# Loading q, k and v with casting DMAs instead of casting them on GpSimd and VectorE

## The chip, the cores and the metric

The kernel runs on one core of one Trainium2 chip. The metric is the device time of one execution in microseconds (us), lower is better. Every time below is a median of executions. Kernels are compared only within the same rounds. A ratio is the mean time of one kernel's runs over that of the other's of the same rounds, so it is not quite the ratio of the medians quoted.

Names of the engines: PE is TensorE (matmuls), PEld its weight loads, DVE is VectorE, ACT is ScalarE, POOL is GpSimd, SP is SyncE.

## The reference

Eight batches of sliding-window attention with an ALiBi bias feed an RWKV channel mix. Cut to what matters:

```python
# q, k, v: (8 batches, 8 heads, 576 positions, 64), float32
scores = q @ k.T / 8 ; scores += -slope[h] * |i - j| ; keep 0 <= i - j < 128
attn = softmax(scores) ; x = attn @ v            # -> (8, 576, 512)
xk = mu_k * x + (1 - mu_k) * x_prev               # x_prev: x of the position before
xr = mu_r * x + (1 - mu_r) * x_prev
out = sigmoid(xr @ w_r) * (relu(xk @ w_k) ** 2 @ w_v)   # w_k 512x1024, w_v 1024x512
```

## The kernel before

The work is cut into 32 iterations, four pairs of heads for each of eight batches. Iterations 0 to 3 (batch 0) have their own code; from iteration 8 on, one loop does everything. In an iteration TensorE transposes q and k of a later pair, computes the scores, ScalarE takes the exponential, VectorE multiplies it by a table of `exp(bias)` and zeros (the "mask multiply"), TensorE multiplies by v (`av`), VectorE normalises (`xu`), TensorE transposes back (`outT`), and VectorE mixes with the position before (`dl`, `xk`, `xr`). Matmuls of the channel mix fill the rest of TensorE's time as `units`.

The inputs come in fp32 by plain DMAs from SyncE. GpSimd casts q and v to bf16, and VectorE casts k:

```python
def cast_qk(it, part=None, fq=pool_cast, fk=vec_cast):
    cs = csp.tile([128, 2, NF, 2, D], BF16, tag="cs", name="cs", bufs=4)
    ...
    for i, f in ((0, fq), (1, fk)):            # q on GpSimd, k on VectorE
        f(cs[:, i, 0:r1 - r0]..., ldr[:, i, it % NBUF]...)

def cast_v(it, j0=0, j1=NF):
    pool_cast(vs_buf[it % NBUF]..., vdr[:, it % NBUF, :, j0:j1])

def feed(it, fk=vec_cast):
    cast_qk(it, None, pool_cast, fk)
    cast_v(it)
    load_qk(it + 4)                            # plain DMAs, rows of 1 KB
    load_v(it + 4)
    if it % G == 0:
        load_tail(it // G + 1)                 # positions 512 to 575
```

The multiply, and the place of `feed` in the loop:

```python
# scores():
nc.scalar.activation(out=ah, in_=sa[:, :, 0:w], func=AF.Exp, scale=float(scale))
if not early:
    nc.vector.tensor_tensor(out=ah, in0=ah,
                            in1=mask[:, 2 * g:2 * g + 2, m0:m0 + w], op=ALU.mult)

# ahead of the loop
feed(2 * G + 2)
...
for it in range(2 * G, NIT + 2):
    scores_full(it)
    run_units(bud * .3)
    if it > 2 * G:
        av(it - 1, 0, NJ)                      # frees at and vs of iteration it - 1
    run_units(bud * .3)
    ...
    transp(it + 2)                             # ends in ScalarE's copy of qk
    feed(it + 3)
    ...
    outT(it - 1, 0, NJ)
```

The order of TensorE, SyncE and GpSimd in the loop is the order of the program; that of VectorE and ScalarE is chosen by the scheduler.

The softmax here doesn't subtract the row's maximum and nothing guards it: scores larger than these inputs give would overflow.

## Time and profile before

The kernel took 274.94 us, the median of three runs (273.6 to 275.26). The profiled run spans 272.5 us. TensorE is busy nearly all the time, and VectorE is second:

| | before |
|---|---|
| TensorE busy | 244.9 us of 272.5 (90%) |
| VectorE busy | 211.4 us (78%) |
| ScalarE, GpSimd busy | 179.9 us, 74.0 us |
| first transposes of iterations 4, 8, 9, 12, 28 | 41.1, 55.4, 67.4, 86.2, 202.2 us |
| mask multiply, mean of 34 in 90 to 210 us | 1048 ns |

The row of first transposes is when TensorE starts the first transpose matmul of an iteration, read from the list of TensorE's instructions in the trace. Four iterations are one batch, so the time from iteration 12 to 28 over four is the steady period: (202.2 - 86.2) / 4 = 29.0 us.

First, the page of the kernel before: busy time of each engine, two rows of the busy tenths in 40 slices (each digit is one slice of about 6.8 us), and the queue of the DMAs that GpSimd issues (packets, MB, share of 16 engines).

```profile
PE 244.9 (90%) x2272; PEld 145.0 (53%) x2304; DVE 211.4 (78%) x428; ACT 179.9 (66%) x293; POOL 74.0 (27%) x121
...
PE   4589899857999899999999999999999999999994
...
PEclk9999999977999999999999999999999999999999
...
q0 software_dynamic: 2160, 2.63, 5.8%
```

TensorE is full from the eleventh slice on. In slices 9 and 10 (about 55 to 68 us) it is at 5 and 7 tenths, and the clock that it was granted falls below 0.8. The windows view splits that stretch at the first transposes of iterations 8, 9 and 12; its columns are the stretch, its length, the busy time and count of each engine, the granted clock (1 is full), the DMA share and the rate.

```profile
core 0: us, PE busy (x) PEld busy (x) DVE busy (x) ACT busy (x) POOL busy (x), PEclk, DMA share, GB/s
55.40:67.40 12.00, 7.32 (x77) 4.84 (x78) 9.39 (x19) 4.23 (x5) 2.84 (x5) 0.72 0.92 241
67.40:86.20 18.80, 17.69 (x174) 10.71 (x175) 15.73 (x30) 14.42 (x21) 3.73 (x6) 1.00 0.71 194
```

Iteration 8 takes 12.00 us for 7.32 us of TensorE work at a clock of 0.72; the next three together take 18.80 us at full clock. The timeline of that stretch (start, duration, engine, line, operation, tiles; in brackets the idle time before it and what ended it) shows what TensorE stood still for:

```profile
55.46 0.68 DVE L130 CAST cs<-ldr 128x512 bf16<-128x512 f32 x1 [3.98 <-DMA ldr<-in_k_dram]
56.06 0.44 DVE L298 TENSOR_TENSOR dl<-xt 128x576 bf16<-128x576 bf16 x1
...
57.27 0.81 DVE L300 SCALAR_TENSOR_TENSOR xr<-dl,mur_sb,xt 128x576 bf16<-128x576 bf16 x1
...
58.46 0.82 DVE L270 TENSOR_TENSOR xu<-sa,rc 128x640 bf16<-128x640 f32 x1
...
59.34 0.71 PE L284 MATMUL to<-ident,xu 128*128 128x128 bf16 x5 [3.30 <-DVE xu L270]
```

VectorE ran these in the order of its queue: ScalarE's copy `xt`, which `dl` reads, was done at 53.59, but the k cast ahead of it waited for a DMA until 55.46. So `dl`, `xr` and `xu` behind it come late, and TensorE stands still 3.30 us for `xu`.

The view of waits of TensorE's weight loads adds such waits up over 90 to 206 us (line, what it waited for: us in total, times, longest):

```profile
PEld L284 <- DVE xu L270: 5.1, 11, 0.6
PEld L262 <- issue: 4.8, 10, 0.6
PEld L312 <- issue: 2.8, 5, 0.7
PEld L341 <- DVE kk L318: 1.6, 3, 0.7
```

The lines that end in "issue" wait for nothing that the profile shows. The two that name VectorE come to 6.7 us.

### The profile page before, as it was taken

Reading aid. Unit: us, or ns where it says so; the run is one execution under the profiler, and the core shown is the slowest. Engines: PE = TensorE matmul, PEld = TensorE weight load, DVE = VectorE, ACT = ScalarE, POOL = GpSimd, SP = SyncE. Lnnn points to the kernel's source line nnn. Section 1 sums busy time; section 2 is a strip of 40 time slices with the busy share of each in tenths; the row PEclk is TensorE's granted clock in tenths of the full one; section 3 lists DMA queues with packets and bytes.
Section 4 is the critical chain, followed back from the end, with each engine's and each line's share of the span. In section 5 each row is a group of like instructions: output and inputs, shape, how many; then the busy total and the mean of one; then the engine's idle time right before and its main releaser. Section 6 shows DMA issues by size and latency. Waiting matters only on the chain.

```text
span 272.5 us, 6003 instructions
## 1 busy us (share of the span) xinstructions
PE 244.9 (90%) x2272; PEld 145.0 (53%) x2304; DVE 211.4 (78%) x428; ACT 179.9 (66%) x293; POOL 74.0 (27%) x121
## 2 busy tenths in 40 slices
PE   4589899857999899999999999999999999999994
PEld 1245665525555565545555755555565755455461
DVE  2268973367878999998988899989888888976342
ACT  5468688832795776876686677866685868635350
POOL 5383066513042225222320225222422100000000
PEclk9999999977999999999999999999999999999999
DMA  6999999998593691791686551972501211022122
GB/s 164 226 206 196 241 246 283 247 295 196 160 282 85 177 265 45 191 243 50 195 207 161 154 161 58 232 196 91 177 2 38 81 38 41 0 81 77 38 79 77
DMA packets 73229, 40.77 MB, mean 150 GB/s; under 512 B 48112, under 2 KB 68080, under 8 KB 73200
## 3 DMA queue, kind: packets, MB, share of 16 engines
q1 hardware_dynamic: 71040, 37.76, 51.8%
q0 software_dynamic: 2160, 2.63, 5.8%
q8 instruction: 18, 0.29, 0.5%
q14 instruction: 11, 0.09, 0.1%
HBM read 33.56 MB, written 9.44 MB: 158 GB/s over the span
## 4 chain that ended last, share of the span: by engine, by line
PE 54%; DVE 15%; ACT 11%; DMA 8%; SPq 5%; issue 5%; POOL 2%; DVEq 0%; POOLq 0%; ACTq 0%
PE pv L341 17%; PE ps L312 14%; PE pr L327 8%; PE sa L262 5%; DMA ldr<-in_k_dram 4%; DVE at L235 4%; ACT at L233 4%; ACT xt L289 3%; PE tp L184 3%; DVE xk L300 2%; DMA vdr<-in_v_dram 2%; ACT rl L316 2%; PE sa L230 2%; DVE xr L300 2%; DMA tq<-in_k_dram 2%
## 5 line engine op out<-in xcount | busy, mean ns | idle before, releaser
L312 PE MATMUL ps<-xk,wk_sb 128*128 128x256 bf16 (+2 forms) x413 | 70.7, 313 | 3.9 <-ACT rl L316 1.5
L341 PE MATMUL pv<-wv_sb,kk 128*128 128x512 bf16 x271 | 68.8, 382 | 1.8 <-issue 0.6
L233 ACT ACTIVATE at<-sa 128x1024 bf16<-128x1024 f32 (+1 forms) x68 | 63.7, 983 | 9.3 <-PE sa L230 9.1
L316 ACT ACTIVATE rl<-ps 128x256 bf16<-128x256 f32 (+2 forms) x104 | 47.8, 478 | 22.1 <-PE ps L312 14.3
L126 POOL TENSOR_SCALAR vs<-vdr 128x512 bf16<-128x512 f32 (+1 forms) x36 | 24.6, 686 | 127.8 <-issue 89.6
L312 PEld LDWEIGHTS <-wk_sb 128*128 128x128 bf16 x416 | 38.6, 97 | 25.3 <-issue 6.1
L235 DVE TENSOR_TENSOR at<-at,mask 128x1024 bf16<-128x1024 bf16 x48 | 44.6, 968 | 0.8 <-ACT at L233 0.8
L318 DVE TENSOR_TENSOR kk<-rl 128x256 bf16<-128x256 bf16 (+2 forms) x104 | 35.6, 362 | 10.8 <-ACT rl L316 8.6
L341 PEld LDWEIGHTS <-kk 128*128 128x128 bf16 x288 | 26.1, 98 | 27.8 <-DVE kk L318 2.0
L332 ACT ACTIVATE rs<-pr 128x512 bf16<-128x512 f32 x36 | 21.7, 606 | 24.2 <-PE pr L327 24.2
L347 DVE SCALAR_TENSOR_TENSOR ot<-rs,pv 128x512 f32<-128x512 bf16 x36 | 24.3, 674 | 16.8 <-PE pv L341 16.3
L327 PE MATMUL pr<-wr_sb,xr 128*128 128x512 bf16 x132 | 35.7, 379 | 0.7
L187 ACT COPY qk<-tp 128x1024 bf16<-128x1024 bf16 x28 | 28.4, 1016 | 10.9 <-PE tp L184 10.6
L126 POOL TENSOR_SCALAR cs<-ldr 128x512 bf16<-128x512 f32 (+1 forms) x38 | 29.5, 777 | 7.7 <-DMA ldr<-in_q_dram 6.7
L262 PEld LDWEIGHTS <-at 128*128 128x128 bf16 x576 | 23.8, 102 | 11.9 <-issue 7.6
L300 DVE SCALAR_TENSOR_TENSOR xk<-dl,muk_sb,xt 128x576 bf16<-128x576 bf16 (+2 forms) x36 | 27.1, 753 | 1.2
L300 DVE SCALAR_TENSOR_TENSOR xr<-dl,mur_sb,xt 128x576 bf16<-128x576 bf16 (+2 forms) x36 | 27.3, 759 | 0.0
L298 DVE TENSOR_TENSOR dl<-xt 128x576 bf16<-128x576 bf16 (+2 forms) x36 | 15.8, 440 | 9.6 <-ACT xt L289 9.3
L270 DVE TENSOR_TENSOR xu<-sa,rc 128x640 bf16<-128x640 f32 x28 | 22.7, 814 | 0.3
L262 PE MATMUL sa<-vs,at 128*128 128x65 bf16 x448 | 19.7, 196 | 2.3 <-ACT at L233 1.6
L230 PE MATMUL sa<-qk 64*128 64x256 bf16 (+1 forms) x264 | 21.2, 268 | 0.6 <-ACT qk L200 0.2
L130 DVE CAST cs<-ldr 128x512 bf16<-128x512 f32 (+1 forms) x30 | 12.4, 414 | 11.9 <-DMA ldr<-in_k_dram 11.9
(56 smaller groups left out, 217.3 us busy)
## 6 DMA issues: line engine op xcount, KB each, us to landing
out_dram<-ot SPq DMA_DIRECT2D x36, 256.0 KB, 2.1
ldr<-in_q_dram SPq DMA_DIRECT2D x29, 256.0 KB, 4.2
ldr<-in_k_dram SPq DMA_DIRECT2D x29, 256.0 KB, 4.5
vdr<-in_v_dram SPq DMA_DIRECT2D x56, 128.0 KB, 3.9
vdr<-in_v_dram SPq DMA_DIRECT2D x4, 256.0 KB, 5.6
tq<-in_q_dram SPq DMA_DIRECT2D x8, 128.0 KB, 4.8
tq<-in_k_dram SPq DMA_DIRECT2D x8, 128.0 KB, 4.9
tv<-in_v_dram SPq DMA_DIRECT2D x8, 128.0 KB, 4.9
```

The costliest lines, as they stand in the source:

```text
L126: nc.gpsimd.tensor_scalar(out=dst, in0=src, scalar1=1.0, scalar2=0.0, op0=ALU.mult, op1=ALU.add)
L187: nc.scalar.copy(out=qk_buf[it % NBUF].rearrange("p t (c r) -> p t c r", r=NF), in_=tp.rearrange("p (t r c) -> p t c r", t=2, r=NF))
L230: nc.tensor.matmul(sa[:, hl, c0:c0 + n], lhsT=kk_, rhs=qq_, start=not early, stop=True, skip_group_check=True)
L233: nc.scalar.activation(out=ah, in_=sa[:, :, 0:w], func=AF.Exp, scale=float(scale))
L235: nc.vector.tensor_tensor(out=ah, in0=ah, in1=mask[:, 2 * g:2 * g + 2, m0:m0 + w], op=ALU.mult)
L262: nc.tensor.matmul(a5[:, hl, t - t0], lhsT=at[:, lo:lo + 128], rhs=vs[:, u, hl, :] if u < NF else tvb[:, 2 * g + hl], start=(u == us[0]), ...
L300: nc.vector.scalar_tensor_tensor(out=dst[:, g, S * e + c0:S * e + c1], in0=dl[:, 0:c1 - c0], scalar=mu[:, g:g + 1], in1=xp, op0=ALU.mult, ...
L312: nc.tensor.matmul(ps[:, 0:n], lhsT=wk_sb[:, po, 128 * fo:128 * fo + 128], rhs=xk[:, po, c0:c1], start=(po == 0), stop=(po == NPO - 1))
L316: nc.scalar.activation(out=rl[:, 0:n], in_=ps[:, 0:n], func=AF.Relu, scale=RELU_SCALE)
L318: nc.vector.tensor_tensor(out=kk[:, fo, 0:n], in0=rl[:, 0:n], in1=rl[:, 0:n], op=ALU.mult)
L327: nc.tensor.matmul(pr, lhsT=xr[:, po, 128 * c:128 * c + 128], rhs=wr_sb[:, po], start=(po == 0), stop=(po == NPO - 1))
L341: nc.tensor.matmul(pv, lhsT=kk[:, fo, o:o + 128], rhs=wv_sb[:, fo], start=(fo == 0), stop=(fo == NFO - 1))
```

## The change

From batch 1 on, q, k and v are loaded by DMAs that cast on the way, issued by GpSimd straight into bf16 buffers of a whole batch. The intent is to take the casts off GpSimd and VectorE. The Trainium skill, "DMA: Bandwidth & Descriptors", section "SWDGE vs HWDGE vs iDMA", gives the reason for the engine: a cast during a DMA is to be had only from GpSimd. The diff, cut to its core:

```diff
-    vs_buf = [cst.tile([128, NF, 2, W], BF16, name=f"vs{i}") for i in range(NBUF)]
+    vs_buf = [cst.tile([128, NF, H, W], BF16, name=f"vs{i}") for i in range(2)]
+    cb_buf = [ldr....bitcast(BF16)[...] for i in range(2)]     # q and k of a batch
...
+    def cast_load_qk(b, i):
+        hs = (q, k)[i][b, :, 0:SM].rearrange("h (p r) d -> p h r d", p=128)
+        for r in range(NF):
+            nc.gpsimd.dma_start(out=cb_buf[b % 2][:, i, r], in_=hs[:, :, r])
+
+    def cast_load_v(b):
+        for j in range(NF):
+            nc.gpsimd.dma_start(out=vs_buf[b % 2][:, j, :, 0:D],
+                in_=v[b, :, 128 * j:128 * j + 128].rearrange("h p d -> p h d"))
+        ...                                    # and the tails, positions 512 to 575
...
     def transp(it):
-        cs = T.pop(("cs", it, None))
+        cs = cb_buf[b % 2]
...
-    def feed(it, fk=vec_cast):
-        cast_qk(it, None, pool_cast, fk)
-        cast_v(it)
-        load_qk(it + 4)
-        load_v(it + 4)
-        ...
+    def feed(b, g):
+        if g == 1:
+            cast_load_v(b + 1)
+        if g == 2:
+            cast_load_qk(b + 2, 0)
+        if g == 3:
+            cast_load_qk(b + 2, 1)
+            cast_load_tail(b + 2)
...
-    feed(2 * G + 2)
```

Each of these DMAs moves 128 partitions x 8 heads = 1024 rows of 64 values, 256 bytes read and 128 written.

More of the change, by code (lines that the diff above doesn't have):

```diff
@@ L52 @@
     cst = ctx.enter_context(tc.tile_pool(name="cst", bufs=1))
-    tlp = ctx.enter_context(tc.tile_pool(name="tlp", bufs=2))
+    tlp = ctx.enter_context(tc.tile_pool(name="tlp", bufs=1))
     csp = ctx.enter_context(tc.tile_pool(name="csp", bufs=3))
@@ L69 @@
     qk_buf = [cst.tile([128, 2, SM], BF16, name=f"qk{i}") for i in range(NBUF)]
-    vs_buf = [cst.tile([128, NF, 2, W], BF16, name=f"vs{i}") for i in range(NBUF)]
+    vs_buf = [cst.tile([128, NF, H, W], BF16, name=f"vs{i}") for i in range(2)]
+    cb_buf = [ldr.rearrange("p i s h c -> p (i s h c)").bitcast(BF16)[:, 4096 * i:4096 * i + 4096].rearrange("p (i r h d) -> p i r h d", i=2, r=NF, h=H) for i in range(2)]
     at_buf = [cst.tile([128, 2 * 1024 + 64], BF16, name=f"at{i}") for i in range(NBUF)]
@@ L98, in load_qk, with cast_load_tail @@
             dst = ldr[:, i, s0:s0 + npair].rearrange("p s h c -> p (s h) c")
-            if part is None:
-                nc.sync.dma_start(
-                    out=dst,
-                    in_=hs[:, 0:SM].rearrange("h (p r) d -> p h (r d)", p=128))
-            else:
-                nc.sync.dma_start(
-                    out=dst[:, :, 128 * part:128 * part + 128],
-                    in_=hs[:, 256 * part:256 * part + 256].rearrange(
-                        "h (p r) d -> p h (r d)", p=128))
+            nc.sync.dma_start(
+                out=dst[:, :, 128 * part:128 * part + 128],
+                in_=hs[:, 256 * part:256 * part + 256].rearrange(
+                    "h (p r) d -> p h (r d)", p=128))
+    def cast_load_qk(b, i):
+        if not 1 <= b < B:
+            return
+        hs = (q, k)[i][b, :, 0:SM].rearrange("h (p r) d -> p h r d", p=128)
+        for r in range(NF):
+            nc.gpsimd.dma_start(out=cb_buf[b % 2][:, i, r], in_=hs[:, :, r])
+    def cast_load_v(b):
+        if not 1 <= b < B:
+            return
+        for j in range(NF):
+            nc.gpsimd.dma_start(
+                out=vs_buf[b % 2][:, j, :, 0:D],
+                in_=v[b, :, 128 * j:128 * j + 128].rearrange("h p d -> p h d"))
+        nc.gpsimd.dma_start(out=tv_buf[b % 2][0:64, :, 0:D],
+                            in_=v[b, :, SM:S].rearrange("h p d -> p h d"))
+    def cast_load_tail(b):
+        if not 1 <= b < B:
+            return
+        ts = csp.tile([128, H, D], BF16, tag="ts", name="ts", bufs=2)
+        T["ts", b] = ts
+        for src, dst in ((q, ts[0:64]), (k, ts[64:128])):
+            nc.gpsimd.dma_start(out=dst, in_=src[b, :, SM:S].rearrange("h p d -> p h d"))
     def load_v_block(b, j):
@@ L113, in load_v_block @@
             in_=v[b, :, 128 * j:128 * j + 128, :].rearrange("h p d -> p h d"))
-    def load_v(it, j0=0, j1=NF):
-        if not 0 <= it < NIT:
-            return
-        b, g = divmod(it, G)
-        for hl in range(2):
-            nc.sync.dma_start(
-                out=vdr[:, it % NBUF, hl, j0:j1],
-                in_=v[b, 2 * g + hl, 128 * j0:128 * j1, :].rearrange(
-                    "(j p) d -> p j d", p=128))
     def pool_cast(dst, src):
@@ L137, in cast_qk @@
             return
-        cs = csp.tile([128, 2, NF, 2, D], BF16, tag="cs", name="cs", bufs=4)
+        cs = csp.tile([128, 2, 2, 2, D], BF16, tag="cs", name="cs", bufs=4)
         T["cs", it, part] = cs
@@ L148, in cast_v @@
             return
-        vs = vs_buf[it % NBUF]
-        pool_cast(vs[:, j0:j1, :, 0:D].rearrange("p j h d -> p h j d"),
+        b, g = divmod(it, G)
+        pool_cast(vs_buf[b % 2][:, j0:j1, 2 * g:2 * g + 2, 0:D].rearrange("p j h d -> p h j d"),
                   vdr[:, it % NBUF, :, j0:j1])
@@ L180, in transp @@
             return
-        cs = T.pop(("cs", it, None))
+        b, g = divmod(it, G)
+        cs = cb_buf[b % 2]
         tp = p_tp.tile([128, 1024], BF16, tag="tp", name="tp")
@@ L185, in transp @@
                 tp[:, 128 * n:128 * n + 128],
-                cs[:, n // NF, n % NF].rearrange("p h d -> p (h d)"), ident)
+                cs[:, n // NF, n % NF, 2 * g:2 * g + 2].rearrange("p h d -> p (h d)"), ident)
         nc.scalar.copy(
@@ L248, in av @@
         b, g = divmod(it, G)
-        at, vs, tvb = at_buf[it % NBUF], vs_buf[it % NBUF], tv_buf[b % 2]
+        at, vs, tvb = at_buf[it % NBUF], vs_buf[b % 2], tv_buf[b % 2]
         nt = t1 - t0
@@ L263, in av @@
                         a5[:, hl, t - t0], lhsT=at[:, lo:lo + 128],
-                        rhs=vs[:, u, hl, :] if u < NF else tvb[:, 2 * g + hl],
+                        rhs=vs[:, u, 2 * g + hl, :] if u < NF else tvb[:, 2 * g + hl],
                         start=(u == us[0]), stop=(u == t), skip_group_check=True)
@@ L440 @@
     make_dist()
+    for i in range(2):
+        nc.gpsimd.memset(vs_buf[i][:, :, :, D], 1.0)
     for i in range(NBUF):
-        nc.gpsimd.memset(vs_buf[i][:, :, :, D], 1.0)
         nc.gpsimd.memset(at_buf[i][:, 2048:2112], 1.0)
@@ L506 @@
     outT(*span(2 * G - 2))
-    nc.gpsimd.tensor_copy(out=ldr[:, :, 0, 0, 0:1], in_=wr_sb[:, 0:2, 0:1])
-    load_qk(G)
-    load_tail(1, (0, 1))
-    load_v(G)
-    load_tail(1, (2,))
-    for g in range(1, G):
-        load_qk(G + g)
-        load_v(G + g)
+    cast_load_qk(1, 0)
+    cast_load_qk(1, 1)
+    cast_load_tail(1)
+    cast_load_v(1)
     def first1(c0, fo):
@@ L520, in first1 @@
             make_mask(range(fo, fo + 1))
-    def feed(it, fk=vec_cast):
-        cast_qk(it, None, pool_cast, fk)
-        cast_v(it)
-        load_qk(it + 4)
-        load_v(it + 4)
-        if it % G == 0:
-            load_tail(it // G + 1)
+    def feed(b, g):
[6 more added lines that the diff above has]
+            cast_load_tail(b + 2)
     for c0 in (0, 256):
@@ L542 @@
     run_units(1800)
-    feed(G, pool_cast)
-    cast_tail(1)
     run_units(1800)
     transp(G)
-    feed(G + 1, pool_cast)
+    cast_load_qk(2, 0)
+    cast_load_qk(2, 1)
     transp_tail(1)
+    cast_load_tail(2)
     run_units(1000)
@@ L562 @@
             av(it - 1, 0, NJ)
-        feed(it + 2, pool_cast)
+        feed(1, g)
         run_units(bud * .5)
@@ L568 @@
     order.__enter__()
-    cast_tail(2)
     av(2 * G - 1, 0, NJ)
@@ L596 @@
         transp(it + 2)
-        feed(it + 3)
-        if g == 1:
-            cast_tail(b + 1)
+        feed(b, g)
         run_units(bud * .4)
```

## The prediction

> **What bounds it now.** TensorE: 244.9 of 272.5 us busy (busy table), matmuls back to back from about 67 us on. Before that, loads pace it. The windows view of 41-67 us shows TensorE busy 20.2 of 26 us at a granted clock of 0.87, DMA share 1.03. The chain of waits there runs through DMA landings and GpSimd casts: tq<-k 45.7-50.6, ldr<-k 51.5-55.4, then VectorE's k cast, which blocks its in-order queue; TensorE stands still 3.3 us from 56.0, and the clock is granted at half for about 6.8 us after it. From 93 us to 225 us VectorE is a near second: 26.2, 23.5, 23.8, 24.0 and 23.9 us busy in windows of 26-27 us.
>
> **Removed.** GpSimd casts: about 60 of its 74 us. VectorE: 22 k casts at 0.41 us, 9-10 us. Also contention: the trace's mask multiplies (line 235) take 0.685 us when no GpSimd cast overlaps (9 of 48), about 1.03 us when one does (39); kk squares 0.29 against 0.57. The Trainium skill, "SBUF — State Buffer", section "Who interferes with whom", says a VectorE instruction with two SBUF inputs contends with a GpSimd instruction that reads SBUF; the trace agrees. That frees another 15 us or so (39 x 0.35, and a few kk).
>
> **Added.** 105 casting DMAs, issued by GpSimd: today's three weight loads cost 0.76-0.91 us of issue each, so about 14 us per batch of GpSimd, idle otherwise. q and k go from 1 KB packets to 256 B rows: 13,824 rows a batch. The cost per row is the open question: casting packets took 98 ns for 2 KB and 173 ns for 4 KB of source, but overlap (share 1.12-1.17), so 13-32 ns per 256 B row is my estimate; less if rows share a packet. That is 11-28 us of DMA a batch against about 29 us of TensorE (first transposes 86, 114, 144, 173, 202 us).
>
> **Moved.** Batch 1's transposes now need all eight q/k DMAs of the batch instead of one pair. They are issued after batch 0's v casts (22.6 us) but queue behind the weights, whose last packets end at 32.8 us. At 18 ns they land at about 43.5 us, where transposition starts at 41.1 today; at 32 ns about 50. Batch 2 then lands at 60 (needed about 55-60).
>
> **Sum (estimate).** Start: stalls of +1 to +5 us (more at 32 ns). Gained back: the 3.3 us hole and half-clock stretch, about 6 us. Steady state: shorter mask multiplies and no casts in VectorE's chain, but TensorE is nearly full, so 25 us of VectorE give 3-5 us. Net -6 us: **268 us**, range 259-288. Chances: faster 0.46, same 0.29, slower 0.25.
>
> **Signs.** Right: no TENSOR_SCALAR casts on GpSimd after 23 us; mask multiply mean near 0.69; VectorE busy near 187; no DMA wait on VectorE; TensorE gap only near 41-45 us (transposes waiting for in_k); period near 28 us; queue 0 carrying most packets, at 10-20 ns each of engine time. Wrong: transposes or scores waiting for DMA at every batch, DMA share near 1 until late, clock dropping to half.
>
> **What would make it wrong.** A casting 256 B row costing 30 ns or more: batches then arrive every 28-31 us, TensorE starves each batch, 285-305 us. Or GpSimd writing descriptors much slower for small rows than 0.9 us per DMA, or held off by VectorE: same symptom with idle DMA engines. The other way, rows packed together: 260-263 us.

## More of the kernel before

In the steady part, the groups of instructions by form between 90 and 210 us (line, engine, operation, tiles, count; busy time, mean ns; idle before) show the two GpSimd casts and the mask multiply:

```profile
L126 POOL TENSOR_SCALAR cs<-ldr 128x512 bf16<-128x512 f32 x17 | 16.4, 963 | 0.0
L126 POOL TENSOR_SCALAR vs<-vdr 128x512 bf16<-128x512 f32 x17 | 13.7, 803 | 86.9 <-issue 68.2 <-DVE xr L300 12.6 <-DMA vdr<-in_v_dram 6.1
...
L235 DVE TENSOR_TENSOR at<-at,mask 128x1024 bf16<-128x1024 bf16 x34 | 34.3, 1048 | 0.0
```

And the timeline of one iteration shows how they lie:

```profile
119.31 0.98 POOL L126 TENSOR_SCALAR vs<-vdr 128x512 bf16<-128x512 f32 x1 [5.21 <-issue]
119.72 2.12 DVE L235 TENSOR_TENSOR at<-at,mask 128x1024 bf16<-128x1024 bf16 x2
...
120.26 1.04 POOL L126 TENSOR_SCALAR cs<-ldr 128x512 bf16<-128x512 f32 x1
...
121.76 0.41 DVE L318 TENSOR_TENSOR kk<-rl 128x512 bf16<-128x512 bf16 x1
...
122.22 0.10 PEld L341 LDWEIGHTS <-kk 128*128 128x128 bf16 x1 [0.71 <-DVE kk L318]
```

The v cast starts when `av` has freed its buffer, the q cast follows at once, and both fall on the two mask multiplies, which take 2.12 us instead of about 1.3. The square `kk` queued behind them ends late, and TensorE's next weight load, which needs it, has waited 0.71 us.

## The result, and the profile after

The changed kernel took 266.41 us (265.69 to 267.03, four runs) against 274.81 us of the kernel before beside it (four runs): ratio 0.9691 [0.9659, 0.9723], so 3.1% faster. A second set of five rounds gave the same:

> The changed kernel again, as the yardstick of the three runs beside it: 0.969 of the kernel before, mask multiply 0.684 us each.

Measured: 266.54 us, ratio 0.9687 [0.9656, 0.9719]. So a small change in an experiment can be told from this kernel down to about 1 us.

The page after:

```profile
PE 239.7 (91%) x2272; PEld 144.2 (54%) x2304; DVE 190.1 (72%) x406; ACT 180.0 (68%) x293; POOL 102.9 (39%) x147
...
PE   4489799977999999999999999999999999999993
...
PEclk9997999999999999999999999999999999999999
...
q0 software_dynamic: 100608, 15.02, 83.1%
```

VectorE lost 21 us of work. GpSimd gained 29 us: most of its casts went, but issuing a DMA counts as busy on it, and 110 issues of 0.7 to 0.9 us make 97 us. The clock no longer drops in slices 9 and 10. (The drop in slice 4, at 19 to 23 us, is in this profile and not in that of after_again, which is the same kernel.) Queue 0 went from 2,160 packets to 100,608. The same two stretches, from the first transposes of iterations 8, 9 and 12:

```profile
55.10:63.20 8.10, 5.05 (x77) 3.54 (x78) 6.77 (x15) 4.23 (x5) 7.94 (x10) 1.00 2.70 152
63.20:82.00 18.80, 17.69 (x174) 10.71 (x175) 13.99 (x28) 14.42 (x21) 8.27 (x11) 1.00 1.21 106
```

Iteration 8 now takes 8.10 us instead of 12.00 for the same 77 matmuls, at full clock; the next three take 18.80 us, as before. So the whole gain of the early part lies in this one iteration: TensorE's work in it went from 7.32 to 5.05 us (the clock, 2.3 us), its idle time from 4.68 to 3.05 us (the hole, 1.6 us). The timeline answers to the one of before:

```profile
53.36 0.46 DVE L310 TENSOR_TENSOR dl<-xt 128x576 bf16<-128x576 bf16 x1 [2.12 <-ACT xt L301]
...
56.09 0.82 DVE L282 TENSOR_TENSOR xu<-sa,rc 128x640 bf16<-128x640 f32 x1
...
56.97 0.45 PE L296 MATMUL to<-ident,xu 128*128 128x128 bf16 x5 [1.27 <-DVE xu L282]
```

No VectorE instruction waits for a DMA. `dl` runs as soon as ScalarE has delivered, and TensorE waits 1.27 us for `xu` instead of 3.30.

In the steady part the mask multiply is at one length, and the waits of the weight loads for VectorE are nearly gone (90 to 210 and 90 to 206 us):

```profile
L247 DVE TENSOR_TENSOR at<-at,mask 128x1024 bf16<-128x1024 bf16 x34 | 21.9, 684 | 0.0
```

```profile
PEld L274 <- issue: 4.9, 9, 0.6
PEld L324 <- issue: 1.0, 3, 0.5
PEld L296 <- DVE xu L282: 0.3, 1, 0.3
```

From the first transposes in the two profiled runs, the 7.7 us between the spans are placed as follows:

| stretch | before | after | difference |
|---|---|---|---|
| start to iteration 8 | 55.4 | 55.1 | -0.3 |
| iterations 8 to 12 | 30.8 | 26.9 | -3.9 |
| iterations 12 to 28 (four periods) | 116.1 | 112.1 | -4.0 |
| iteration 28 to the end | 70.2 | 70.7 | +0.5 |
| span | 272.5 | 264.8 | -7.7 |

Two gains of 4 us each are to be explained. I did not follow the half microsecond at the end.

### The profile page after: what moved, and what is told of

Its sections match the earlier page's. It is cut to its first block, busy times and chain, and to the rows that moved or that the text cites. A ratio compares the mean times of both kernels' runs of the same rounds, so it can differ in the third digit from the quotient of the medians.

```text
span 264.8 us, 5798 instructions
## 1 busy us (share of the span) xinstructions
PE 239.7 (91%) x2272; PEld 144.2 (54%) x2304; DVE 190.1 (72%) x406; ACT 180.0 (68%) x293; POOL 102.9 (39%) x147
## 4 chain that ended last, share of the span: by engine, by line
PE 60%; ACT 13%; DMA 11%; DVE 7%; issue 3%; POOL 3%; SPq 1%; POOLq 0%; DVEq 0%; ACTq 0%
PE pv L353 20%; PE ps L324 16%; PE pr L339 10%; ACT at L245 6%; DMA wv_sb<-in_moe_w_v_dram 6%; PE sa L274 5%; PE tp L196 4%; ACT xt L301 3%; DMA ts<-in_k_dram 3%; DMA vdr<-in_v_dram 2%; PE sa L242 2%; ACT rl L328 2%; PE tp L296 2%; DVE xk L312 2%; ACT qk L199 1%
## 5 line engine op out<-in xcount | busy, mean ns | idle before, releaser
L353 PE MATMUL pv<-wv_sb,kk 128*128 128x512 bf16 x271 | 67.7, 379 | 1.2 <-issue 0.5
L328 ACT ACTIVATE rl<-ps 128x256 bf16<-128x256 f32 (+2 forms) x104 | 47.6, 477 | 18.3 <-PE ps L324 13.6
L330 DVE TENSOR_TENSOR kk<-rl 128x256 bf16<-128x256 bf16 (+2 forms) x104 | 33.6, 337 | 16.6 <-ACT rl L328 14.4
L116 POOL DMA_DIRECT2D vs<-in_v_dram x28 | 24.8, 908 | 42.4 <-PE sa L274 41.3
L110 POOL DMA_DIRECT2D ldr<-in_q_dram x28 | 25.1, 917 | 24.3 <-PE tp L196 24.3
L247 DVE TENSOR_TENSOR at<-at,mask 128x1024 bf16<-128x1024 bf16 x48 | 31.0, 684 | 0.8 <-ACT at L245 0.8
L274 PEld LDWEIGHTS <-at 128*128 128x128 bf16 x576 | 22.6, 99 | 12.0 <-issue 7.5
L312 DVE SCALAR_TENSOR_TENSOR xr<-dl,mur_sb,xt 128x576 bf16<-128x576 bf16 (+2 forms) x36 | 26.9, 748 | 0.0
L110 POOL DMA_DIRECT2D ldr<-in_k_dram x28 | 24.8, 924 | 4.4 <-DMA wv_sb<-in_moe_w_v_dram 3.6
L274 PE MATMUL sa<-vs,at 128*128 128x65 bf16 x448 | 18.9, 193 | 3.0 <-ACT at L245 2.6
```

The costliest lines, as they stand in the source:

```text
L110: nc.gpsimd.dma_start(out=cb_buf[b % 2][:, i, r], in_=hs[:, :, r])
L247: nc.vector.tensor_tensor(out=ah, in0=ah, in1=mask[:, 2 * g:2 * g + 2, m0:m0 + w], op=ALU.mult)
L274: nc.tensor.matmul(a5[:, hl, t - t0], lhsT=at[:, lo:lo + 128], rhs=vs[:, u, 2 * g + hl, :] if u < NF else tvb[:, 2 * g + hl], start=(u == ...
L312: nc.vector.scalar_tensor_tensor(out=dst[:, g, S * e + c0:S * e + c1], in0=dl[:, 0:c1 - c0], scalar=mu[:, g:g + 1], in1=xp, op0=ALU.mult, ...
L328: nc.scalar.activation(out=rl[:, 0:n], in_=ps[:, 0:n], func=AF.Relu, scale=RELU_SCALE)
L330: nc.vector.tensor_tensor(out=kk[:, fo, 0:n], in0=rl[:, 0:n], in1=rl[:, 0:n], op=ALU.mult)
```

## The experiments

Theory A: the steady 4.0 us come from GpSimd's casts no longer lying on the mask multiplies. The Trainium skill, "SBUF — State Buffer", section "Who interferes with whom", states that a VectorE instruction with two inputs in SBUF contends with a GpSimd instruction that reads SBUF, but not with one that only writes. The mask multiply has two such inputs. In the timeline of before the two casts and two multiplies fill 119.31 to 121.84 us, 2.5 us; alone two multiplies take about 1.3 us and two casts 2 x 0.61 us, together also 2.5 us. So they took as long as if they ran one at a time. The single multiplies say the same: of the 48 in the trace 33 took 1.09 to 1.10 us and 15 took 0.68 to 0.69 and none took a time in between. VectorE's `ot`, whose second input lies in PSUM (TensorE's output memory), took 0.67 to 0.68 us beside a cast or not. But having two inputs is not the only case: three k casts with one input (at 55.46, 107.91 and 166.95 us), each beside a GpSimd cast, took 0.68 to 0.71 us instead of 0.41.

Theory B: VectorE's k casts were in TensorE's way, and taking them off VectorE gave the 4 us. Theory C: neither; the loads, the buffers or the order of the queues did it. For the early 3.9 us, the theory is the one of the prediction: the k cast that waits for a DMA at the head of VectorE's queue.

Stretches of all runs, each from one profiled run, beside the times. "Casts" is the summed time of GpSimd's casts in 90 to 210 us, and "multiply" the mean of the mask multiply there.

| run | casts, us | multiply, ns | iterations 8 to 12 | 12 to 28 | period | time, us | ratio to before |
|---|---|---|---|---|---|---|---|
| before | 37.5 | 1048 | 30.8 | 116.1 | 29.02 | 274.8 to 275.1 | 1 |
| e1_hole | 37.4 | 1048 | 29.0 | 116.0 | 29.01 | 272.18 | 0.9897 |
| e11_aside | 33.1 | 683 | 30.3 | 112.8 | 28.20 | 269.74 | 0.9808 |
| after_again | 0 | 684 | 26.6 | 112.1 | 28.03 | 266.54 | 0.9687 |
| e2_read | 22.0 | 684 | 27.0 | 112.2 | 28.04 | 266.34 | 0.9695 |
| e3_write | 3.0 | 685 | 26.6 | 112.1 | 28.03 | 266.33 | 0.9695 |
| e4_dve | 0 | 684 | 26.5 | 112.1 | 28.03 | 266.15 | 0.9685 |
| e5_both | 24.3 | 685 | 26.6 | 112.5 | 28.13 | 266.99 | 0.9707 |
| e9_memset | 0 | 685 | 26.8 | 112.1 | 28.03 | 266.73 | 0.9691 |
| e8_overlap | 33.3 | 1069 | 26.8 | 115.8 | 28.95 | 271.19 | 0.9852 |
| e10_putback | 32.5 | 1017 | 26.6 | 116.9 | 29.22 | 271.44 | 0.9869 |
| e7_qk_only | 14.4 | 808 | 27.7 | 115.1 | 28.78 | 279.62 | 1.0152 |
| e6_double | 0 | 685 | 33.3 | 112.1 | 28.03 | 280.06 | 1.0176 |

### e4_dve: only VectorE's cast work put back

The kernel after, with a needless cast of the size of the k cast on VectorE in each iteration of the loop:

```diff
         feed(b, g)
+        if it < NIT - 2:
+            vec_cast(jb[:, 2048:2560], jq[(it + 2) % NBUF])   # reads qk as fp32
```

> The changed kernel with one useless VectorE cast per iteration from batch 2 on (22 of about 0.4 us, fp32 to bf16, 128x512), no GpSimd casts. If removed cast work on VectorE carried the steady-state gain: +2 us or more. If contention did: 0 to +1.5 us.

Measured: 266.15 us (ratio 0.9685 [0.9654, 0.9715]), period 28.03. The work was done, as the groups of 90 to 210 us show:

```profile
L144 DVE CAST vdr<-qk 128x512 bf16<-128x512 f32 x16 | 8.2, 510 | 1.5 <-ACT qk L202 1.3
```

Putting 22 casts, 11 us of VectorE, back into this kernel cost nothing. Theory B falls for this kernel: there VectorE has idle time in which they fit.

### e2_read, e3_write, e5_both: a dose that missed

Two needless GpSimd casts per iteration (e2), memsets of about the same length (e3), and e2 with e4 together (e5). All were held back until ScalarE's copy of qk was made:

```diff
         feed(b, g)
+        if it < NIT - 2:
+            src = jq[(it + 2) % NBUF]                 # qk as fp32
+            for z in range(2):                        # e2; e3: one small cast, then
+                pool_cast(jb[:, 512 * z:512 * z + 512], src)    # two memsets
```

> The changed kernel with two useless GpSimd casts per iteration (fp32 to bf16, 128x512, reading SBUF) from batch 2 on, 44 in all. Contention theory: mask multiplies that overlap one take about 1.05 us again, VectorE busy rises by 6 to 15 us, time +2 to +4 us (ratio 0.977 to 0.984), all of it after 67 us. Rival (the steady-state gain came from removed VectorE cast work or from earlier data, not from contention): mask multiply may slow, but the time stays within 0.8 us of the changed kernel.

> The same, but the GpSimd work only writes SBUF: two memsets per iteration of about the same length, with one 2-element cast ahead of them to pin their place. Contention[...]: mask multiply stays near 0.69 us and time within 0.8 us of the changed kernel. If any GpSimd work slows VectorE (or delays the DMA issues): the same cost as in the run with casts.

> The changed kernel with both useless loads together from batch 2 on: two GpSimd casts and one VectorE cast per iteration. If the theory is complete (hole plus contention plus cast work), this gives back the steady-state part: +3 to +5 us against the changed kernel, ratio 0.980 to 0.988, with the early part (first transposes of batch 2 at about 55 to 63 us) still as in the changed kernel. If something else (whole-batch prefetch) carried the steady part: under +1.5 us.

Measured: 266.34, 266.33 and 266.99 us. The timeline of e2 shows why this told nothing about theory A:

```profile
123.87 1.20 POOL L140 TENSOR_SCALAR vdr<-qk 128x512 bf16<-128x512 f32 x2 [5.54 <-ACT qk L202]
...
127.29 1.29 DVE L250 TENSOR_TENSOR at<-at,mask 128x1024 bf16<-128x1024 bf16 x2
```

The casts ran at 123.87 to 125.07, two microseconds ahead of the next mask multiplies, and the multiply stayed at 684 ns. An experiment that adds the suspected cost must be read at the instruction that should suffer before its time is read. What these runs do say: two GpSimd casts an iteration that don't lie on the multiplies cost nothing.

### e8_overlap, e9_memset, e10_putback: the dose where it belongs

In e8 the needless casts overwrite the `at` buffer that `av` has just read, so they wait for the same event as the v cast of before did. e9 does the same with memsets, and e10 adds e4's VectorE cast. The outputs stay correct, since `at` is written anew before it is read again.

```diff
+        if 2 * G < it < NIT - 2:
+            ja = at_buf[(it - 1) % NBUF]
+            for z in range(2):
+                pool_cast(ja[:, 1024 * z:1024 * z + 512],       # e9: memset
+                          jv[:, 512 * z:512 * z + 512])
         feed(b, g)
```

> The kernel after, with two needless GpSimd casts (128x512, fp32 to bf16) put back in each of iterations 9 to 29; this time each is held back until the attention-times-v matmuls have read the at buffer that it overwrites, which is when the kernel before ran its v cast, so that they fall on the mask multiplies (the earlier try, held behind ScalarE's copy of qk, fell beside them). The mask multiply should go from 684 back to about 1000 ns in the steady part; if it does not, the run says nothing again. Theory A (a GpSimd cast beside a mask multiply lengthens the multiply, and that delay reaches TensorE through the at tiles and the queue behind them; these casts are where the about 4 us of steady lead came from): the period grows from 28.0 to 28.7 or more, time 268.5 to 270.5 us. Theory B (VectorE has slack in the steady part, so freeing it was worth nothing and the steady lead comes from something else, such as the cs buffers or the k cast's place in VectorE's queue): 266.0 to 267.2 us, period 28.0.

> The same places and the same pin as in the run with two overlapping GpSimd casts, but as memsets, which write the same 128x512 bf16 and read nothing. It tells whether it is GpSimd being busy, or its reads of memory together with VectorE's, that lengthens the mask multiply. If reads: multiply stays at about 685 ns and the time at 266.0 to 267.2 us. If any GpSimd work does it: the multiply rises above 800 ns, and the time with it.

> Both: the two overlapping GpSimd casts per iteration and one VectorE cast of 128x512 per iteration behind ScalarE's copy of qk, so about the engine work of the kernel before in the steady part, with the loads of the kernel after. Theory A with the VectorE work adding to it: 269.0 to 271.5 us, period 28.7 to 29.1 (before: 29.0). If it stays at 266 to 267.2 the steady lead has nothing to do with engine time, and lies in the loads, the buffers or the order of the queues.

Measured: e8 271.19 us (0.9852 [0.9816, 0.9888]), e9 266.73 us (0.9691 [0.9656, 0.9726]), e10 271.44 us (0.9869 [0.9838, 0.9900]). The groups and the timeline of e8, and then the waits of its weight loads:

```profile
L138 POOL TENSOR_SCALAR at<-vdr 128x512 bf16<-128x512 f32 x32 | 32.9, 1041 | 37.0 <-PE sa L275 37.0
...
L248 DVE TENSOR_TENSOR at<-at,mask 128x1024 bf16<-128x1024 bf16 x32 | 33.0, 1069 | 0.0
```

```profile
115.05 2.12 POOL L138 TENSOR_SCALAR at<-vdr 128x512 bf16<-128x512 f32 x2 [1.34 <-PE sa L275]
115.59 2.11 DVE L248 TENSOR_TENSOR at<-at,mask 128x1024 bf16<-128x1024 bf16 x2
```

```profile
PEld L297 <- DVE xu L283: 3.7, 9, 0.6
PEld L354 <- DVE kk L331: 1.1, 3, 0.5
```

The multiply is back at 1069 ns, the waits for `xu` and `kk` are back (4.8 us, before 6.7, after 0.3), and the period is 28.95 us. The time rose by 271.19 - 266.54 = 4.7 us (4.5 by the ratios, since the two ran in different rounds); at 271.19 it is above the 268.5 to 270.5 that theory A had set for it. The groups of e9 show about as many pieces of GpSimd work in the same places, which only write. Each takes 523 ns, a little less than a cast alone (0.61 us):

```profile
L609 POOL MEMSET at<- 128x512 bf16 x34 | 16.7, 523 | 58.0 <-PE sa L275 58.0
...
L248 DVE TENSOR_TENSOR at<-at,mask 128x1024 bf16<-128x1024 bf16 x34 | 21.9, 685 | 0.0
```

The multiply stayed at 685 ns and the time where it was. It is not GpSimd being busy, and not the extra wait that the pin brings, but GpSimd work that reads SBUF while VectorE reads two tiles from it. This is what the skill's page says. e10 adds to e8 a VectorE cast that cost nothing in e4. In the stretch from iteration 12 to 28 it costs 116.9 - 115.8 = 1.1 us here, from iteration 12 to the end 188.2 - 187.5 = 0.7 us, and in the times 0.25 us, inside the spread of the runs. So work on VectorE begins to cost, if at all, only once the contention has filled it.

### e11_aside: the casts kept, but moved

The reverse test starts from the kernel before, with its loads and casts. A two-element GpSimd cast that reads qk holds each iteration's casts back until after the multiplies. It contains the edit of e1 too (below).

```diff
+    pin = cst.tile([128, 2], BF16, name="pin")
-    feed(2 * G + 2)
+    pool_cast(pin, jq[(2 * G + 1) % NBUF][:, 0:2])
+    feed(2 * G + 2, pool_cast)
...
+        if it + 3 < NIT:
+            pool_cast(pin, jq[(it + 2) % NBUF][:, 0:2])
         feed(it + 3)
```

> The kernel before, loads and casts kept, with two edits: the k cast of iteration 10 on GpSimd (as in the earlier run of that alone, 272.2 us), and in the steady part a two-element GpSimd cast that reads ScalarE's copy of qk just ahead of each iteration's GpSimd casts, so that they start after that copy and fall beside VectorE work other than the mask multiplies. Theory A (the steady gain of the change is the end of GpSimd casts lying on the mask multiplies, and nothing else): mask multiply about 690 to 750 ns in the steady part, period 28.0 to 28.2, time 267.0 to 268.5 us, without one casting DMA. Rival C (the steady gain needs the casts and their loads to be gone, for example because the q and k casts hold up the transposes once they start later): multiply falls but the period stays above 28.5 and the time at 270 us or more. It beats the kernel after only if it is under 266 us, which I do not expect, since about 1 us of the start is left.

Measured: 269.74 us (268.15 to 271.24), ratio 0.9808 [0.9768, 0.9848]. The steady part did what theory A expected: multiply 683 ns, period 28.20, iteration 12 to the end 183.1 us against 186.3 before and 182.8 after. GpSimd still spent 33.1 us in casts there, and all k casts but that of iteration 10 were still on VectorE. So theories B and C fall for 3.3 of the 4.0 us: these came without any change of the loads. What makes up the other 0.7 us was not separated. VectorE did not even become less busy in 90 to 210 us: 111.0 us, before 111.1, after 98.7. The casts now lengthened other work, such as the square `kk` of 128x384 (540 ns on average, before 344), and that cost little. So in this kernel it is the place of the lengthened instruction that counts, and not how much time VectorE has left. The time missed the expectation of 267.0 to 268.5 us. The miss lies mostly in iterations 8 to 12 (30.3 us, in e1 29.0), where the hole opened again, 3.27 us. Its timeline shows the reason:

```profile
52.91 2.37 DVE L300 TENSOR_TENSOR dl<-xt 128x576 bf16<-128x576 bf16 x1 [1.79 <-ACT xt L291]
...
53.19 0.62 POOL L128 TENSOR_SCALAR vs<-vdr 128x512 bf16<-128x512 f32 x1
53.77 1.19 POOL L128 TENSOR_SCALAR cs<-ldr 128x512 bf16<-128x512 f32 x2
```

`dl`, which takes 0.46 us alone and also reads two tiles, took 2.37 us: three GpSimd casts ran on top of it.

### e1_hole: only the cast that waits

The kernel before, with one k cast moved from VectorE to GpSimd: that of iteration 10, which waited for its DMA at 55.46 us.

```diff
-    feed(2 * G + 2)
+    feed(2 * G + 2, pool_cast)
```

> The kernel before with one cast moved: k of iteration 10 is cast by GpSimd instead of VectorE, so VectorE's queue no longer stands behind that DMA at 51.5-55.4 us. Theory: the 3.3 us TensorE hole at 56 us and the half-clock stretch after it go, 3 to 4.5 us faster (ratio 0.984 to 0.989), and the first transposes of later batches move by the same amount, not more. Rival (the hole is the latency of the attention chain itself, or the next cast blocks in its place): within 1 us of before.

Measured: 272.18 us, ratio 0.9897 [0.9873, 0.9921], 2.7 us under the 274.8 us of before in its rounds: less than the 3 to 4.5 us expected, more than the rival's 1 us. By the trace, iterations 8 to 12 fell from 30.8 to 29.0 us, 1.8 of the 3.9; the hole fell from 3.30 to 2.55 us and the half clock from 6.8 to 3.4 us. `dl` no longer waited for a DMA, but took 1.29 us and `xr` 1.16 us, with GpSimd's casts beside them, against 0.46 and 0.81 after:

```profile
53.73 1.29 DVE L298 TENSOR_TENSOR dl<-xt 128x576 bf16<-128x576 bf16 x1 [2.21 <-ACT xt L289]
...
55.19 2.24 POOL L126 TENSOR_SCALAR cs<-ldr 128x512 bf16<-128x512 f32 x2 [0.47 <-DMA ldr<-in_q_dram]
...
55.79 1.16 DVE L300 SCALAR_TENSOR_TENSOR xr<-dl,mur_sb,xt 128x576 bf16<-128x576 bf16 x1
```

One of the two casts beside `xr` is the k cast itself, which this edit moved to GpSimd, so the 1.8 us may be less than the blocked queue cost. The hole had a second cause behind the first, and e11 shows the same one. That these slower instructions make up all of the remaining 2.1 us is argued from the two timelines. A run of before with the casts of the start kept off `dl` was not made.

### e6_double: twice the casting rows

Every casting DMA over 128 partitions is issued a second time, into a scratch tile.

```diff
         for r in range(NF):
             nc.gpsimd.dma_start(out=cb_buf[b % 2][:, i, r], in_=hs[:, :, r])
+            again(hs[:, :, r])                # and the same for v
```

> The changed kernel with each of its 84 128-partition casting DMAs issued twice, the second into a scratch buffer nothing reads: about 23 us of issue per batch instead of 13. If the casting path has room in steady state, only the start pays: batch 1's transposes 6 to 8 us later, batch 2's later still by 5 to 10, total +8 to +20 us, and batch periods from batch 3 on unchanged near 28 us. If the path is nearly full already, every batch period grows and the time exceeds 300 us. Mean issue time of a DMA tells whether GpSimd (0.88 us each) or the DMA engines (issues waiting on landings) pace it.

Measured: 280.06 us, ratio 1.0176 [1.0147, 1.0206], 13.5 us over the kernel after. The steady period is 28.03, as after, and only the start pays: iteration 8 begins at 62.0 instead of 55.1 us, iterations 8 to 12 take 33.3. TensorE then waits for the k loads one after another (waits of TensorE, 41 to 76 us):

```profile
PE tp L206 <- DMA ldr<-in_k_dram: 8.0, 6, 1.5
```

This gives the cost of a row. Nearly every issue still took 0.87 to 0.98 us of GpSimd, and once the weights had landed its data came in 4.7 to 6.6 us after it was issued, without that delay growing along a run of some 50 DMAs: the DMA engines kept up. In the kernel after, the first seven q and k DMAs were issued while the weights were still landing; when these were through, they landed 0.84 to 0.88 us apart most of the time (33.12, 33.99, 34.84). So a DMA of 1024 rows costs about 0.87 us at both ends, issue and engines, or 0.87 / 64 = 13.6 ns per row on each of 16 engines. Here the landings did not merely follow the issues: the eighth of these DMAs was issued 4.5 us after the seventh (32.56 and 28.06), yet landed 0.84 us after it. Nor does the issue go with the rows: a tail of 512 rows was issued in 0.68 to 0.78 us. Which of the two sets the pace where DMAs are issued without a pause can't be told from this.

### e7_qk_only: half of the change

q, k and the tails by casting DMAs, v as before (plain DMAs from SyncE, cast by GpSimd):

```diff
     def cast_load_v(b):
-        for j in range(NF):
-            nc.gpsimd.dma_start(out=vs_buf[b % 2][:, j, :, 0:D], ...)
+    def feed_v(it):
+        cast_v(it)
+        load_v(it + 4)
```

> Half of the change: only q, k and the tails come by casting DMA; v as before, plain DMAs from SyncE and a GpSimd cast per iteration. Theory: the early hole stays away, half of the contention comes back (mask multiply mean about 0.80 to 0.90 us), 1 to 2.5 us slower than the full change. Rival (v's casting loads are the ones that crowd GpSimd and the DMA queue): as fast as the full change or faster.

Measured: 279.62 us, ratio 1.0152 [1.0123, 1.0181]: slower than either kernel, where 1 to 2.5 us over the full change had been expected. Of the 11.3 us between the spans of this profile and of after, 7.6 lie before iteration 8 and 3.0 between iterations 12 and 28. The waits of TensorE at 39 to 56 us show where the early part arises:

```profile
PE tp L206 <- DMA ldr<-in_k_dram: 2.4, 4, 0.7
PE tp L206 <- DMA ldr<-in_q_dram: 2.3, 3, 1.4
```

In the kernel after no such wait is in this window. The second q DMA is issued at the same time in both (22.97 and 23.02 us), but lands at 39.86 instead of 33.99 us, while the plain loads of v, issued by SyncE (nine of 128 KB between 22 and 46 us), take their turn on the same engines. This agrees with the skill's "DMA: Bandwidth & Descriptors", section "Issuing engines are not separate DMA queues". That these loads are the whole reason is not shown. The steady part is a further point for theory A: with half the casts the multiply is at 808 ns and the period at 28.78.

## Why the prediction was right, and where it was off

The call (faster, 268.0 us, within 259 to 288) held: 266.41 us. Its terms, one by one:

- **"Start: stalls of +1 to +5 us"** was mis-sized. The start to iteration 8 measured -0.3 us. I had taken 18 ns per row; the measured pace is 13.6 ns. The last k DMA of batch 1 landed at 39.7 us, not 43.5, and the tail at 41.1 us; TensorE waited 0.3 us there. The rows did not share packets either: queue 0 carried about 96,800 packets of 128 bytes, one for each row. e6 shows what twice the cost would have done: over 13 us, all in the start. So the named danger was real, and less than twice the cost per row would have brought it. The estimate had been 13 to 32 ns, and 18 was picked from it without a reason; that the cost came out at the low end was luck.
- **"Gained back: the 3.3 us hole and half-clock stretch, about 6 us"** measured 3.9 us. The clock term was nearly right (2.3 us, where 6 - 3.3 leaves 2.7), the hole term was too large: TensorE's idle time in iteration 8 fell by 1.6 us, not 3.3, since it still waits 1.27 us for `xu`, and at the next `xu` 1.57 us instead of 1.00. Of the cause that I named, "VectorE's k cast, which blocks its in-order queue", e1 confirms 1.8 us; behind it lay `dl` and `xr` beside GpSimd casts, which I had not seen, because in before `dl` starts too late to meet them.
- **"25 us of VectorE give 3-5 us"** came to 4.0 us, but as a sum it was wrong reasoning. It put the end of the contention (some 15 us) and of the k casts (9 to 10 us) into one pool. The first is worth nearly all of it: e8 puts back 3.7 of 4.0 us in iterations 12 to 28, and e11 gains 3.3 us without the change. The second was worth nothing in the kernel after (e4). What counts is which instruction is lengthened: the mask multiply stands ahead of `kk` and `xu`, which TensorE's next weight loads need. e11 shows it: most of the gain came with VectorE as busy as before.
- **The sum** came within 1.6 us of the measured time partly by luck: the start was put 1 to 5 us too high and the early gain 2 us too high, and the two errors work against each other.
- **Signs.** Mask multiply 0.684 us, period 28.03, no DMA wait on VectorE after batch 0, no casts on GpSimd in the steady part, most packets on queue 0: as predicted. VectorE's busy time was 190 us, predicted 187. The gap at 41 to 45 us shrank to 0.3 us; the larger ones, 1.27 and 1.57 us, lie at 57 and 62 us and wait for `xu`. One sign named for "wrong" appeared and meant nothing: the DMA share was 1.08 to 1.21 from 67 to 172 us. The packets' records overlap, so a share near 1 did not mean that TensorE had to wait.

Open: whether GpSimd's issue or the DMA engines set the 0.87 us where DMAs are issued without a pause; the 0.5 us at the end; the 0.7 us that e11 lacks; and the part of the early 3.9 us that e1 leaves. e8 costs somewhat more than the change had gained (187.5 us from iteration 12 to the end, before 186.3). That excess lies after iteration 28 (71.7 us, before 70.2), where 5 of 10 multiplies were lengthened in e8 and 2 in before; between 12 and 28 it was 30 of 32 and 29. I did not test it further.

## What to carry to other kernels

A second engine's work is not free because that engine is idle: look where it lies in time, and what the other engine reads at that moment. Here two GpSimd casts an iteration cost about 4 us on top of two-input VectorE multiplies and nothing where they ended 2 us ahead of them (e2), and one small instruction that pinned their start gained most of what the casting DMAs did in the steady part. Before a change moves loads to casting DMAs of small rows, count the rows, at 0.87 us for 1024 of 256 bytes here, and ask by when the first batch must have landed.

## What the Trainium skill lacked or had wrong

- "DMA: Bandwidth & Descriptors", section "Anatomy of one DMA", calls descriptor generation a small, variable part of the fixed cost. For a casting DMA of 1024 rows GpSimd was busy mostly 0.87 to 0.98 us per issue, which is not small, though 512 rows took 0.68 to 0.78, so it grows little with the rows. The landings came at 0.84 to 0.88 us. No page gives the time of a casting row (13.6 ns on each of 16 engines, while the trace's packet records of these rows are 32 ns long and overlap); the section "Why small descriptors are slow" of the same page counts cycles for a plain 256-byte descriptor and does not speak of casts.
- "SBUF — State Buffer", section "Who interferes with whom": its rule on two-input VectorE instructions and reading or only writing GpSimd work was right (multiply 1069 ns beside casts, 685 ns beside memsets). What it lacks is the size on real kernels: a multiply of 684 ns became one of 1087 to 1103 ns, one `dl` of 460 ns became 2365 ns beside three casts.
- "TensorE: Matmul & The Clock Gate", Part 1, has the clock halve after an idle window of about 3.4 us. Here a hole of 2.55 us (e1) was followed by 3.4 us of half clock, and one of 3.30 us (before) by 6.8 us, which began 1.8 us into the hole; a hole of 1.57 us (after) had no such effect. But the length of a hole did not decide alone: in after the clock was halved for 3.4 us from 19.4 us, at a hole of 0.86 us, and in after_again, at one of 1.13 us in the same place, it was not. TensorE was sparsely busy around these holes, so they need not contradict the page, but in this kernel a gap under 3.4 us was no safe gap.
- No page says that casting loads split with plain ones can be worse than either alone: half of this change took 279.6 us, the whole 266.5, none 274.9.
